# Packing a batch's transform into the first third of its tiles, so that the second third can use two-product values

## The chip, the cores and the metric

The kernel runs on one core of one Trainium2 chip. The metric is the device time of one execution in microseconds (us). The engines are named as in the profile: PE is TensorE (matrix products; PEld its weight loads), DVE is VectorE, ACT is ScalarE, POOL is GpSimd, SP is SyncE, whose queue issues most transfers. PSUM is the accumulator memory that PE writes; this kernel uses all eight of its banks of 128 x 512 float32.

## The reference

Eight batches of 3008 x 256 go through a two-dimensional Fourier transform whose real part is kept, and then row by row through a gated feed-forward layer of width 1536.

```python
def _attn_ref(x):                      # x: (8, 3008, 256)
    X = np.fft.fft(x, axis=1)
    X = np.fft.fft(X, axis=2)
    return X.real.astype(np.float32)

def _moe_ref(x, w_gate, w_val, w_out): # x: (24064, 256)
    gate = np.maximum(x @ w_gate, 0.0)
    val = x @ w_val
    return (gate * val @ w_out).astype(np.float32)
```

## The kernel before

**Transform.** The transform over the 3008 rows is computed as matrix products with tables of sines and cosines. It leaves two bf16 tables for each batch, U (cosine part) and V (sine part), with 128 channels on the partitions and 1505 columns. One column stands for two output rows, which differ only in the sign of V's contribution. The transform over the 256 channels is not computed: it is folded into the weights once, which gives WA (weights for U), WB (weights for V) and WM = -2 WB. The channel in the middle sits in a row of its own, CB, and is added as a bias ("seed") by ACT.

A batch's transform is 24 products of 376 or 377 columns, in four *families* of six: V and U for odd outputs, V and U for even outputs. All families accumulate in one PSUM bank, d (pool psD, one buffer). A family's first three products write d; ACT copies d to the tile es (L598); the next three products add to the same bank; ACT copies the total to the table as bf16 (L601, "whole"); DVE computes the mirrored half as 2 es - d in two instructions of 188 columns each (L603, "half-sums"). Only when both half-sums have read d may the next family, or any other user of d, write the bank.

**Feed-forward.** A batch's columns are cut into three *blocks* of 512, 512 and 481 columns (`thirds`). Each block has 12 tiles of 128 hidden units (`fi`). So a batch from 1 on has 36 *slots*, one call of `slot` for each tile, numbered `at` = 12 block + fi. While the tiles of batch b run, the transform of batch b+1 is computed (`todo_dft`), the input of batch b+2 is folded on POOL (`todo_fold`), and the output products of the block before are spread over the slots (`todo_out`, L784, two per 128 x 512 output bank, evicted by ACT at L797).

A usual tile ("n") has five products. Gate: WM0 V into bank g (L1021), copied by ACT as q (L1024); WA0 U onto a seeded bank p (L1028). DVE forms p - q/2 (L1032) and POOL adds q (L1033): these are the gates of the two rows of a column. Value: WA1 U and WB1 V into a bank v (L876, L877), multiplied by the gate on DVE (L912); then WM1 V is added to the same bank (L882, "mirror"), which turns the value into that of the other row, and DVE multiplies again (L912). The mirror is issued in the next slot, when the tile is `pending`, and waits until the first multiplication has read v.

A *short* tile has two value products instead of three: ACT seeds bank d (L1049), WA1 U is added (L1053), ACT copies twice that (L1054), WV V is added (L1058, WV is half of -WM1). The other row's value is the copy minus d, formed on DVE in place where the tile is `own` (L1065), on DVE in SBUF and multiplied on POOL where it is not (L1067, L1068). A "j" tile has its gate in one bank: WA0 U onto the seeded p (L1028), copied doubled by ACT (L1039), WB0 V added (L1043), copied by ACT (L1044), the difference on POOL (L1045). A *mixed* block has short tiles at fi 2 and 8 and j tiles at fi 5 and 11.

Short tiles need bank d, so they stand where no transform does. Before the change these are the third blocks of batches 2 to 5 (mixed), and in batches 6 and 7, where POOL has less to do, the third block of 6 and all of 7 (short tiles at fi 2, 6, 10, or 2, 5, 8).

**The order of work** is written by hand: engines execute in the order in which the code issues. `slot(cur, mid, nxt, after)` works on tiles fi to fi+3: the first part of the output products, the gate products of `nxt`, the seed of `after`, the mirror of `pending` and its multiplication, the value of `cur` and its first multiplication, L1032 and L1033 of `nxt`, one eviction, one half-sum, the rest of the output products (about 3 of 8). After each slot the batch loop issues `DFT_EVEN[at]` transform steps.

```python
DFT_EVEN = (3, 0, 3, 0, 0, 0) * 4 + (0,) * 12
```

So before the change a family takes six slots, and the four families take the first and the second block. Each list of deferred steps is emptied one step at a time: `evict` holds ACT's copies (the transform's go to its front), `sums` the half-sums. `run_fold` issues POOL's folding steps by a credit of 0.72 us per slot.

Of the kernel before, what the change touches and what calls it, by code (L numbers as in the profile page):

```python
# [34 lines left out]
def kernel(  # L35
# [8 lines left out]
    nc = tc.nc  # L44
    B, S, D = x.shape
# [511 lines left out]
            return dst[:, 0:NJ], dst[:, NJ:2 * NJ]  # L557
        return dst[:, 3 * NJ:4 * NJ + 1], dst[:, 2 * NJ:3 * NJ]

    evict, sums = [], []  # L560

    def flush():
        for todo in (evict, sums):
            while todo:
                todo.pop(0)()

# [3 lines left out]
    def family(b, dst, fam, sine, now=True, pool=None):  # L570

        n, cols = (NE, slice(0, NE)) if fam == 0 else (NJ, slice(NE, NK))
        src, tab = (GG[b % 2], tabS) if sine else (FF[b % 2], tabC)
        st, apart = {}, now or pool is not None

        def mm(par, t, nyq=False):
            if par not in st and not apart and not par:
                st[0] = st[1]  # L580
            elif par not in st:
                home, tag = pool or ((psG, "g") if now and not par else (psD, "d"))
                st[par] = home.tile([128, 512], F32, name=tag, tag=tag)
            rows = slice(0, ROWS[par][t])
            if nyq:
                nc.tensor.matmul(st[par][0:1, 0:n], lhsT=FF[b % 2][rows, fam, t, par, 128:129], rhs=tabC[rows, 2 * t + par, cols],
                                 start=False, stop=(t == 2), skip_group_check=True)
            else:
                nc.tensor.matmul(st[par][:, 0:n], lhsT=src[rows, 1 - fam if sine else fam, t, par, 0:128],  # L589
                                 rhs=tab[rows, 2 * t + par, cols], start=(t == 0 and (apart or par == 1)), stop=(t == 2),  # L590
                                 skip_group_check=not apart)
                if b > 2 and (fam, sine, par, t) == (0, False, 0, 2):
                    widen(st[par], n)

        def end(par):
            if par:
                st["es"] = rp.tile([128, NE], F32, name="es", tag="es", bufs=2)
                evict.insert(0, lambda: nc.scalar.copy(st["es"][:, 0:n], st[1][:, 0:n]))  # L598
            elif not apart:
                whole, rest_ = half_of(dst, fam)  # L600
                evict.insert(0, lambda: nc.scalar.copy(whole, st[1][:, 0:n]))  # L601
                for c in (slice(0, NJ // 2), slice(NJ // 2, NJ)):
                    sums.append(lambda c=c: nc.vector.scalar_tensor_tensor(rest_[:, c], in0=st["es"][:, c], scalar=2.0, in1=st[1][:, c],  # L603
                                                                           op0=ALU.mult, op1=ALU.subtract))
            else:
                for d, op in zip(half_of(dst, fam), (ALU.add, ALU.subtract)):
                    m = d.shape[-1]
                    sums.append(lambda d=d, op=op, m=m: nc.vector.tensor_tensor(d, st["es"][:, 0:m], st[0][:, 0:m], op=op))
            if now:
                flush()  # L610

        def at(par):
            home, tag = pool
            st[par] = home.tile([128, 512], F32, name=tag, tag=tag)
            return st[par]
        return mm, end, at

    def dft_first(U, V):

        raw, ends = [], [family(0, dst, 1, False, now=False, pool=pool) for dst, pool in ((U, (psP, "p")), (V, (psO, "o")))]  # L620
        bank = {(k, par): ends[k][2](par) for k in range(2) for par in (1, 0)}

        def products(t, k, rs):
            src, tab = ((FF[1], tabC), (GG[1], tabS))[k]
            for r, par in [(r, par) for r in rs for par in (1, 0)]:
                rows = slice(0, ROWS[par][t])
                nc.tensor.matmul(bank[k, par][:, 0:NJ], lhsT=src[rows, r, t, par, 0:128], rhs=tab[rows, 2 * t + par, odd_k],
                                 start=(t == 0 and r == 0), stop=(t == 2 and r == 1), skip_group_check=bool(k))

        def nyquist(t):  # L630
            for par in (1, 0):
                rows = slice(0, ROWS[par][t])
                nc.tensor.matmul(bank[1, par][0:1, 0:NJ], lhsT=ny[rows, t, par:par + 1], rhs=tabC[rows, 2 * t + par, odd_k],
                                 start=False, stop=False, skip_group_check=True)

        def combine(i, js):
            for j in js:
                home, tag = ((psV, "v"), (psV, "v"), (psG, "g"), (psD, "d"))[len(raw)]
                p = home.tile([128, 512], F32, name=tag, tag=tag)
                for kc in range(2):  # L640
                    nc.tensor.matmul(p[:], lhsT=(TA, TB)[j][:, kc, :], rhs=wr[i][0][:, kc, :], start=(kc == 0), stop=(kc == 1))
                raw.append(p)

        def whole(W, p):
            return W[:, 0:512], p[:]

        products(0, 0, (0,))
        products(0, 1, (0,))
        whole_128(0)
        angle(4, 5)  # L650
        products(0, 0, (1,))
        products(0, 1, (1,))
        nyquist(0)
        angle(5, 4)
        whole_128(1)
        for T in (TA, TB):
            nc.scalar.copy(T[:, 1, 0::2], T[:, 0, 0::2])
            nc.scalar.mul(T[:, 1, 1::2], T[:, 0, 1::2], -1.0)
        products(1, 0, (0, 1))
        products(1, 1, (0, 1))  # L660
        nyquist(1)
        combine(0, (0, 1))
        nc.scalar.copy(*whole(WA[0], raw[0]))
        whole_128(2)
        products(2, 0, (0, 1))
        ends[0][1](1)
        ends[0][1](0)
        evict.pop(0)()
        nc.vector.tensor_scalar(m2[:], pidx[:], scalar1=1.0, op0=ALU.min, scalar2=-2.0, op1=ALU.mult)
        sums[0]()  # L670
        nc.scalar.copy(*whole(WB[0], raw[1]))
        nyquist(2)
        products(2, 1, (0, 1))
        ends[1][1](1)
        ends[1][1](0)
        evict.pop(0)()
        sums[2]()
        combine(1, (0, 1))
        nc.scalar.copy(*whole(WA[1], raw[2]))
        nc.scalar.copy(*whole(WB[1], raw[3]))  # L680
        for k in (1, 3):
            sums[k]()
        del sums[:]
# [160 lines left out]

    DFT_0 = (0, 0, 0, 0, 0, 3, 0, 0, 4, 3, 3, 0), (0, 0, 0, 0, 0) + (1,) * 7, (3, 3, 3, 3, 3, 3, 0, 0, 0, 0, 0, 0)

    DFT_EVEN = (3, 0, 3, 0, 0, 0) * 4 + (0,) * 12
    DFT_1 = (3, 0, 3, 0, 0, 0) * 4 + (0, 1, 0, 1, 1) + (0,) * 7
    todo_out, todo_dft, todo_fold = [], [], []
    credit, paired = 0, False  # L850
# [8 lines left out]
    def run_one(todo):  # L859
        if todo:  # L860
            todo.pop(0)()
# [136 lines left out]
    def new_tiles():  # L998
        for b in range(1, B):
            for blk, block in enumerate(thirds):  # L1000
                for fi in range(NF):
                    st = tile_of(block, fi, uv[b])
                    st["b"] = b
                    mixed = 1 < b < 6 and blk == 2
                    st["kind"] = "o" if (b, blk, fi) == (1, 0, 6) else "j" if mixed and fi in (5, 11) else "n"
                    st["own"] = mixed
                    st["short"] = mixed and fi in (2, 8) or (b, blk) in ((6, 2), (7, 0), (7, 1)) and fi in SHORT or (b, blk) == (7, 2) and fi in (2, 5, 8)
                    st["lead"] = (b, blk, fi) == (1, 0, 0)
                    yield st

    def seed(st):

        if st is None or st["kind"] == "o":
            return
        st["p"] = bank("p")
        nc.scalar.activation(st["p"][:, 0:st["n"]], st["c"], ACTF.Copy, scale=b2[:, st["fi"]:st["fi"] + 1])  # L1016
# [55 lines left out]
    def slot(cur, mid, nxt, after, outs, fold_us):  # L1072
# [7 lines left out]
            run(todo_out, len(todo_out) - stop + outs * part // 8)  # L1080
        old = nxt is not None and nxt["kind"] == "o"
        new = nxt is not None and nxt["kind"] == "n"
        if old:
            gate(nxt)
        lead = cur["lead"]
# [31 lines left out]
        if lead:  # L1117
            out(5)
            cosine_part(nxt)
            seed(after)  # L1120
        if new:
            both(nxt)
        if old:
# [6 lines left out]
        if nxt is not None and nxt["short"]:  # L1130
            seed_value(nxt)
        run_fold(fold_us)
        if not joined:
            run_one(evict)
        run_one(sums)
        out(8)
        return cur

# [3 lines left out]
    for b in range(B):  # L1142
# [4 lines left out]
        for blk, block in enumerate(blocks):  # L1147
# [72 lines left out]
            else:  # L1220
                for fi in range(NF):
# [1 line left out]
                    cur = ahead.pop(0)  # L1223
                    add_h(cur, hs)
                    ahead.append(next(tiles, None))
                    outs = per_tile + ((-2, 0, -2, 2, 2, 0)[fi % 6] if per_tile == 7 else 0)
                    if (b, blk) == (B - 1, 2) and fi > 8:
                        outs = (10, 9, 19)[fi - 9]
                        if fi == 9:
# [5 lines left out]
                        nc.scalar.mul(WV[:, f], WM[1][:, f], -0.5)  # L1235
                    if (b, at) == (2, 0):
                        nc.sync.dma_start(out=WB[0][0:1, :], in_=WM[0][0:1, :])
                    pending = slot(cur, *ahead, outs, .72)
                    for step in more_1.get(at, ()) if b == 1 else ():
                        step()  # L1240
                    run(todo_dft, DFT_1[at] if b == 1 else DFT_EVEN[at])
# [44 lines left out]
```

## Time and profile before

| | us |
|---|---|
| median of 3 runs | 625.35 (625.21 to 625.96) |
| the profiled execution | 625.38 |
| its span, first to last instruction | 623.5 |
| PE busy | 614.8 (99%) |
| DVE busy | 547.9 (88%) |
| POOL busy | 516.4 (83%) |
| ACT busy | 473.6 (76%) |

The profiled execution is 0.03 us from the median; 1.9 us of it lie outside the span. A timeline row gives the start in us from the beginning of the span, the duration of the whole row in us, the engine, the line of the kernel, the operation, the tiles (out<-in), the shape and how many instructions are merged in the row (x3). A bracket at the end names idle time before it and what ended that. A matmul's row shows its latency, which overlaps with the next one, so PE's pace is read from the distance of starts. A row of the stage table gives, for a stretch of the span, the elapsed time, then each engine's busy time (and instruction count), PE's granted clock, the share of the transfer engines and GB/s. A few matmul records are missing from the trace.

The batches from 1 on begin at about 112 us. Batch 2's three blocks run from 187.05 to 211.50, to 236.97 and to 259.60 us, measured at the start of the last value product of the block's last tile.

### The profile page before, as it was taken

What the parts mean: (1) busy time and instruction counts of PE and PEld (TensorE: products, weight loads), DVE (VectorE), ACT (ScalarE), POOL (GpSimd) and SP (SyncE); (2) the same over time, 40 slices, a digit from 0 to 9 for tenths busy, and PEclk for the clock granted to TensorE, in tenths of its full rate; (3) what the DMA queues carried; (4) which work ended last, traced back from release to release, by engine and by line L of the source; (5) the groups of instructions that cost most, each with busy time, mean ns of one, the idle gap of its engine ahead of it and who ended that gap; (6) DMA issues with size and microseconds to landing.
All of it is one profiled execution on the core that took longest, in us unless ns stands there. A gap on an engine that the chain in (4) does not pass through costs nothing.

```text
span 623.5 us, 12412 instructions
## 1 busy us (share of the span) xinstructions
PE 614.8 (99%) x4043; PEld 396.4 (64%) x4087; DVE 547.9 (88%) x978; ACT 473.6 (76%) x878; POOL 516.4 (83%) x490
## 2 busy tenths in 40 slices
PE   8999999999999999999999999999999999999997
PEld 2566666566666666666666666666666666666666
DVE  8886677999899899988999999999999999999991
ACT  7796667777778778776887778777787768999982
POOL 8988992998899988799879989799886656888881
PEclk9999999999999999999999999999999999999999
DMA  9965658744264427315362425211211111211113
GB/s 241 213 200 135 169 181 92 183 88 144 85 152 143 131 71 178 122 45 167 79 189 69 142 77 120 64 54 49 77 44 55 43 61 37 61 52 53 44 51 104
DMA packets 86034, 66.48 MB, mean 107 GB/s; under 512 B 41639, under 2 KB 69063, under 8 KB 85970
## 3 DMA queue, kind: packets, MB, share of 16 engines
q1 hardware_dynamic: 81384, 60.02, 35.4%
q0 software_dynamic: 3984, 4.92, 4.0%
q8 instruction: 32, 0.52, 0.4%
q10 hardware_dynamic: 602, 0.75, 0.4%
q14 instruction: 32, 0.26, 0.1%
HBM read 41.89 MB, written 34.17 MB: 122 GB/s over the span
## 4 chain that ended last, share of the span: by engine, by line
PE 95%; DVE 1%; POOL 1%; issue 1%; DMA 1%; ACT 0%; DVEq 0%; POOLq 0%; ACTq 0%
PE o L784 38%; PE v L882 10%; PE v L877 10%; PE p L1028 8%; PE g L1021 8%; PE v L876 8%; PE d L589 4%; PE p L882 1%; PE p L876 1%; PE p L877 1%; DMA XG<-in_x_dram,gidx 1%; PE d L1053 1%; PE d L1058 1%; PE o L427 1%; POOL XG L120 1%
## 5 line engine op out<-in xcount | busy, mean ns | idle before, releaser
L1033 POOL TENSOR_TENSOR r<-r 128x512 f32<-128x512 f32 (+1 forms) x243 | 302.7, 1253 | 80.2 <-DVE r L1032 77.3
L784 PE MATMUL o<-wo,h 128*128 128x256 bf16 x2172 | 329.6, 273 | 0.2
L912 DVE SCALAR_TENSOR_TENSOR h<-r,v 128x512 bf16<-128x512 f32 (+1 forms) x462 | 294.3, 675 | 38.2 <-PE v L882 32.3
L784 PEld LDWEIGHTS <-h 128*128 128x128 bf16 x2220 | 216.6, 98 | 110.6 <-issue 0.9
L1016 ACT ACTIVATE p<-CB,b 128x512 f32<-128x512 bf16 (+1 forms) x251 | 172.1, 686 | 51.5 <-DVE r L1032 49.6
L1024 ACT COPY r<-g 128x512 f32<-128x512 f32 (+1 forms) x243 | 140.4, 578 | 48.3 <-PE g L1021 41.5
L1032 DVE SCALAR_TENSOR_TENSOR r<-r,p 128x512 f32<-128x512 f32 (+1 forms) x243 | 163.1, 671 | 0.8 <-ACT r L1024 0.8
L877 PE MATMUL v<-V,WB 128*128 128x512 bf16 (+3 forms) x273 | 100.1, 367 | 2.1
L1028 PE MATMUL p<-U,WA 128*128 128x512 bf16 (+1 forms) x251 | 94.1, 375 | 0.0
L1021 PE MATMUL g<-V,WM 128*128 128x512 bf16 (+1 forms) x243 | 91.2, 375 | 0.2
L882 PE MATMUL v<-V,WM 128*128 128x512 bf16 (+1 forms) x232 | 87.0, 375 | 0.2 <-DVE h L912 0.2
L876 PE MATMUL v<-U,WA 128*128 128x512 bf16 (+3 forms) x237 | 86.4, 365 | 0.0
L901 DVE TENSOR_TENSOR h<-r,v 128x376 bf16<-128x376 f32 (+2 forms) x90 | 46.2, 547 | 16.4 <-PE v L882 10.5
L876 PEld LDWEIGHTS <-WA 128*128 128x128 bf16 x328 | 31.9, 97 | 36.1 <-issue 13.4
L797 ACT COPY os<-o 128x512 f32<-128x512 f32 x92 | 52.5, 570 | 2.9 <-issue 2.9
L198 POOL TENSOR_TENSOR XG<-XG,XD 128x510 f32<-128x510 f32 x42 | 52.9, 1268 | 0.8 <-DMA XG<-xr 0.8
L892 ACT ACTIVATE r<-p 128x376 f32<-128x376 f32 (+1 forms) x80 | 38.3, 487 | 18.0 <-PE p L882 8.6
L877 PEld LDWEIGHTS <-WB 128*128 128x128 bf16 x328 | 31.9, 97 | 31.4 <-ACT WB L680 0.2
L206 POOL TENSOR_TENSOR AA<-XG 128x510 f32<-128x510 f32 x42 | 45.3, 1092 | 0.0
L1021 PEld LDWEIGHTS <-WM 128*128 128x128 bf16 x243 | 23.8, 98 | 5.6 <-issue 0.3
L1028 PEld LDWEIGHTS <-WA 128*128 128x128 bf16 x251 | 24.5, 98 | 3.3 <-issue 0.2
L882 PEld LDWEIGHTS <-WM 128*128 128x128 bf16 x233 | 22.8, 98 | 3.6
(201 smaller groups left out, 534.8 us busy)
## 6 DMA issues: line engine op xcount, KB each, us to landing
out_dram<-os SPq DMA_DIRECT2D x124, 128.0 KB
xr<-in_x_dram SPq DMA_DIRECT2D x12, 768.0 KB
XG<-xr SPq DMA_DIRECT2D x12, 768.0 KB
XD<-in_x_dram SPq DMA_DIRECT2D x15, 512.0 KB
out_dram<-os SPq DMA_DIRECT2D x35, 112.0 KB
XD<-in_x_dram SPq DMA_DIRECT2D x8, 448.0 KB
CB<-ch SPq DMA_DIRECT2D x7, 376.2 KB
out_dram<-os SPq DMA_DIRECT2D x13, 96.0 KB
```

Of the source, the lines that this page charges most:

```text
L198: e.tensor_tensor(XG[p, r, t, ::-1, 1:D], XG[p, r, t, ::-1, 1:D], XD[p, r, t, :, D - 1:0:-1], op=ALU.add)
L784: nc.tensor.matmul(st["p"][0:m, q, :], lhsT=lhs(f), rhs=wo[:, f, :], start=(f == 0 and not (early and q)), stop=(f == NF - 1), skip_group_ ...
L876: nc.tensor.matmul(bank[:, 0:st["n"]], lhsT=WA[i][:, st["f"]], rhs=st["us"], start=True, stop=False)
L877: nc.tensor.matmul(bank[:, 0:st["n"]], lhsT=WB[i][:, st["f"]], rhs=st["vs"], start=False, stop=True)
L882: nc.tensor.matmul(bank[:, 0:st["n"]], lhsT=W[i][:, st["f"]], rhs=v, start=False, stop=True, skip_group_check=True)
L912: nc.vector.scalar_tensor_tensor(half_h(st, sign), in0=st["s"][1 + sign][:, 0:n], scalar=0.0, in1=st["v"][:, 0:n], op0=ALU.max, op1=ALU.mult)
L1016: nc.scalar.activation(st["p"][:, 0:st["n"]], st["c"], ACTF.Copy, scale=b2[:, st["fi"]:st["fi"] + 1])
L1021: nc.tensor.matmul(st["g"][:, 0:n], lhsT=WM[0][:, st["f"]], rhs=st["vs"], start=True, stop=True)
L1024: nc.scalar.copy(q[:, 0:n], st["g"][:, 0:n])
L1028: nc.tensor.matmul(st["p"][:, 0:n], lhsT=WA[0][:, st["f"]], rhs=st["us"], start=False, stop=True, skip_group_check=True)
L1032: nc.vector.scalar_tensor_tensor(sp[:, 0:n], in0=q[:, 0:n], scalar=-0.5, in1=st["p"][:, 0:n], op0=ALU.mult, op1=ALU.add)
L1033: nc.gpsimd.tensor_tensor(sm[:, 0:n], sp[:, 0:n], q[:, 0:n], op=ALU.add)
```

## The change

The transform of batch b+1 is issued within the first block of batch b (for b from 2): a family takes three slots, three products after each of two slots and none after the third. Its two ACT copies have a list of their own, `turned_out`, emptied at the start of a slot; a half-sum is issued in the slot after the first multiplication of `cur`, ahead of L1032; after slot 11 one more is issued. With bank d free, the second blocks of batches 2 to 5 become mixed, and the second block of batch 6 gets short tiles at fi 2, 6 and 10. Output products of a first block are spread by -1, -1, +2 over each three slots, and the folding credit per slot becomes 0.76, 0.54, 0.54 us by block. For batch 1 the order stays. The changes in `flush` and `dft_first` only rename the list.

```diff
     def flush():
-        for todo in (evict, sums):
+        for todo in (turned_out, evict, sums):
             while todo:
                 todo.pop(0)()
...
                 st["es"] = rp.tile([128, NE], F32, name="es", tag="es", bufs=2)
-                evict.insert(0, lambda: nc.scalar.copy(st["es"][:, 0:n], st[1][:, 0:n]))
+                turned_out.append(lambda: nc.scalar.copy(st["es"][:, 0:n], st[1][:, 0:n]))
             elif not apart:
                 whole, rest_ = half_of(dst, fam)
-                evict.insert(0, lambda: nc.scalar.copy(whole, st[1][:, 0:n]))
+                turned_out.append(lambda: nc.scalar.copy(whole, st[1][:, 0:n]))
...
-    DFT_EVEN = (3, 0, 3, 0, 0, 0) * 4 + (0,) * 12
+    DFT_EVEN = (3, 3, 0) * 4 + (0,) * 24
...
-                    mixed = 1 < b < 6 and blk == 2
+                    mixed = 1 < b < 6 and blk > 0
...
-                    st["short"] = mixed and fi in (2, 8) or (b, blk) in ((6, 2), (7, 0), (7, 1)) and fi in SHORT or (b, blk) == (7, 2) and fi in (2, 5, 8)
+                    st["short"] = mixed and fi in (2, 8) or (b, blk) in ((6, 1), (6, 2), (7, 0), (7, 1)) and fi in SHORT or (b, blk) == (7, 2) and fi in (2, 5, 8)
...
         new = nxt is not None and nxt["kind"] == "n"
+        early = cur["b"] > 1
+        if early:
+            run_one(turned_out)
         if old:
             gate(nxt)
...
+        if early:
+            run_one(sums)
         if new:
             both(nxt)
...
         run_fold(fold_us)
-        if not joined:
+        if turned_out and not early:
+            run_one(turned_out)
+        elif not joined:
             run_one(evict)
-        run_one(sums)
+        if not early:
+            run_one(sums)
         out(8)
         return cur
...
-                    outs = per_tile + ((-2, 0, -2, 2, 2, 0)[fi % 6] if per_tile == 7 else 0)
+                    if b < 2:
+                        outs = per_tile + ((-2, 0, -2, 2, 2, 0)[fi % 6] if per_tile == 7 else 0)
+                    else:
+                        outs = per_tile + (0 if blk or b == B - 1 else (-1, -1, 2)[fi % 3])
...
-                    pending = slot(cur, *ahead, outs, .72)
+                    pending = slot(cur, *ahead, outs, .72 if b < 2 else (.76, .54, .54)[blk])
+                    if (b > 1 and at == 11):
+                        run_one(sums)
```

Counted in the two built programs, PE has 11 products (and 11 weight loads) fewer, all of 512 columns: 11 tiles become short (33 value products L876, L877, L882 go, 22 products L1053, L1058 come), and 8 products L1021 are replaced by 8 products L1043. DVE has 980 instructions in both. ACT has 33 more, POOL 3 more.

More of the change, by code (lines that the diff above doesn't have):

```diff
@@ L558, in half_of @@
         return dst[:, 3 * NJ:4 * NJ + 1], dst[:, 2 * NJ:3 * NJ]
-    evict, sums = [], []
+    evict, sums, turned_out = [], [], []
     def flush():
-        for todo in (evict, sums):
+        for todo in (turned_out, evict, sums):
             while todo:
@@ L667, in dft_first @@
         ends[0][1](0)
-        evict.pop(0)()
+        turned_out.pop(0)()
         nc.vector.tensor_scalar(m2[:], pidx[:], scalar1=1.0, op0=ALU.min, scalar2=-2.0, op1=ALU.mult)
@@ L675, in dft_first @@
         ends[1][1](0)
-        evict.pop(0)()
+        turned_out.pop(0)()
         sums[2]()
```

## The prediction

> **What bounds the kernel now.** I read the page first: totals, granted clock, and the chain that ended last.
>
> ```profile
> span 623.5 us, 12412 instructions
> ...
> PE 614.8 (99%) x4043; PEld 396.4 (64%) x4087; DVE 547.9 (88%) x978; ACT 473.6 (76%) x878; POOL 516.4 (83%) x490
> ...
> PEclk9999999999999999999999999999999999999999
> ...
> PE 95%; DVE 1%; POOL 1%; issue 1%; DMA 1%; ACT 0%; DVEq 0%; POOLq 0%; ACTq 0%
> ```
>
> PE is the chain, at the full clock. A busy PE is not PE at its peak, so I then read PE's timeline in a first block, over one slot without transform products and into the next.
>
> ```profile
> 203.40 0.65 PE L589 MATMUL d<-tabS,G 128*128 128x377 bf16 x3
> 203.88 0.38 PE L1021 MATMUL g<-V,WM 128*128 128x512 bf16 x1
> 204.10 0.71 PE L784 MATMUL o<-wo,h 128*128 128x256 bf16 x5
> 204.65 0.38 PE L1028 MATMUL p<-U,WA 128*128 128x512 bf16 x1
> 204.86 0.38 PE L882 MATMUL v<-V,WM 128*128 128x512 bf16 x1
> 205.08 0.38 PE L876 MATMUL v<-U,WA 128*128 128x512 bf16 x1
> 205.29 0.38 PE L877 MATMUL v<-V,WB 128*128 128x512 bf16 x1
> 205.51 0.49 PE L784 MATMUL o<-wo,h 128*128 128x256 bf16 x3
> ...
> 206.60 0.38 PE L1028 MATMUL p<-U,WA 128*128 128x512 bf16 x1
> 206.81 0.38 PE L882 MATMUL v<-V,WM 128*128 128x512 bf16 x1
> 207.03 0.38 PE L876 MATMUL v<-U,WA 128*128 128x512 bf16 x1
> 207.25 0.38 PE L877 MATMUL v<-V,WB 128*128 128x512 bf16 x1
> 207.46 0.49 PE L784 MATMUL o<-wo,h 128*128 128x256 bf16 x3
> 207.79 0.48 PE L589 MATMUL d<-tabS,G 128*128 128x377 bf16 x2
> ```
>
> Starts follow without a gap: four 512-column products take 205.51 - 204.65 = 0.86 us, 0.215 each; three output products 207.79 - 207.46 = 0.33, 0.11 each; three transform products 203.88 - 203.40 = 0.48, 0.16 each. So a PE instruction taken out is worth its pace, and a wait put into PE's order is worth its length. Third, the stages: batch 2's blocks, the second block of batch 6, the first of batch 7.
>
> ```profile
> 187.05:211.50 24.45, 24.32 (x158) 15.54 (x160) 22.50 (x39) 19.15 (x35) 24.45 (x22) 1.00 0.48 159
> 211.50:236.97 25.47, 25.36 (x171) 16.65 (x172) 23.82 (x43) 19.41 (x35) 23.20 (x22) 1.00 0.28 76
> 236.97:259.60 22.63, 22.58 (x152) 14.88 (x153) 20.59 (x35) 17.64 (x32) 17.56 (x15) 1.00 0.60 162
> 503.77:529.25 25.48, 25.38 (x171) 16.65 (x172) 23.83 (x43) 20.06 (x36) 16.52 (x14) 1.00 0.19 60
> 551.64:574.63 22.99, 22.83 (x152) 14.90 (x153) 22.09 (x37) 20.95 (x38) 18.70 (x16) 1.00 0.15 48
> ```
>
> After the elapsed time come PE, PEld, DVE, ACT, POOL. DVE follows PE at 92 to 96%, so where a result of DVE is wanted soon, it is late. How DVE stands in a slot, first without, then with half-sums:
>
> ```profile
> 205.35 1.29 DVE L912 SCALAR_TENSOR_TENSOR h<-r,v 128x512 bf16<-128x512 f32 x2 [0.56 <-PE v L882]
> 206.55 0.68 DVE L1032 SCALAR_TENSOR_TENSOR r<-r,p 128x512 f32<-128x512 f32 x1
> 207.30 1.28 DVE L912 SCALAR_TENSOR_TENSOR h<-r,v 128x512 bf16<-128x512 f32 x2
> ```
>
> ```profile
> 225.81 0.65 DVE L1032 SCALAR_TENSOR_TENSOR r<-r,p 128x481 f32<-128x481 f32 x1
> 226.37 0.34 DVE L603 SCALAR_TENSOR_TENSOR U<-es,d 128x188 bf16<-128x188 f32 x1
> 226.63 1.28 DVE L912 SCALAR_TENSOR_TENSOR h<-r,v 128x512 bf16<-128x512 f32 x2
> 227.83 0.65 DVE L1032 SCALAR_TENSOR_TENSOR r<-r,p 128x481 f32<-128x481 f32 x1
> 228.45 1.26 DVE L912 SCALAR_TENSOR_TENSOR h<-r,v 128x512 bf16<-128x512 f32 x2
> ```
>
> The pair L912 (second multiplication of `pending`, first of `cur`) begins 0.49 us after the mirror starts (204.86 to 205.35; 206.81 to 207.30): the mirror's latency and a semaphore. From the pair's start to DVE's next start are 1.20 us (226.63 to 227.83), from a half-sum to the next 0.26, from L1032 to a pair at once behind it 0.62.
>
> **The change part by part.** *PE work removed:* 11 products of 512 columns, 11 x 0.215 = 2.37 us. The 24 transform products of a batch are moved, not removed; the exchange of L1021 for L1043 in 8 tiles is even.
>
> *The packed families.* This is the step on which the result hangs. Now a family's second half-sum stands in the third slot after the family's first, behind that slot's pair; and at that slot's end stand the next family's first products, which overwrite bank d and so wait for this half-sum. Before, two slots lay between:
>
> ```profile
> 200.81 0.34 DVE L603 SCALAR_TENSOR_TENSOR U<-es,d 128x188 bf16<-128x188 f32 x1
> ```
>
> This family's last half-sum ended at 201.15, and the next family's product began at 203.40 (above). Bank d had been free for over 2 us. In the changed order PE runs from the mirror to the transform product in 207.79 - 206.81 = 0.98 us (three products of 512 columns, three of output; each first-block slot at fi 3, 6 and 9 has exactly three left, with 6 or 7 products in all). DVE needs, from the same mirror: 0.49 to the pair, 1.20 through it, the half-sum's 0.34, and the semaphore back to PE. That last step is read where the mirror itself waits for a multiplication:
>
> ```profile
> 229.44 0.37 PE L1028 MATMUL p<-U,WA 128*128 128x481 bf16 x1
> 229.76 0.36 PE L882 MATMUL v<-V,WM 128*128 128x481 bf16 x1
> ```
>
> The pair that began at 228.45 ended at 229.71, and L882 started 0.05 later. So the transform product can start 0.49 + 1.20 + 0.34 + 0.05 = 2.08 us after the mirror, and PE stands for 2.08 - 0.98 = 1.10 us. That is the lower value, for a DVE that is free when the mirror ends. It isn't: the slot before carries the first half-sum, also between pair and L1032. Counted from that slot's mirror, its pair starts at 0.49, half-sum at 1.69, L1032 at 1.95, and the next pair not before 1.95 + 0.62 = 2.57. The next mirror follows after five products of 512 columns and 8 or 7 output products (no transform products in between): 1.95 us by rows (204.86 to 206.81) with 8, 1.84 with 7. The pair so starts 0.62 or 0.73 after its mirror instead of 0.49, and the wait is 1.10 + 0.13 = 1.23 or 1.10 + 0.24 = 1.34 us.
>
> Nothing else covers it: behind the waiting product on PE stand L1021 of the next tile and the five engines' whole supply, and PE executes in its order. It occurs at the second, third and fourth family of a batch (slots 3, 6, 9; the first finds d long free), in batches 2 to 6, 15 times. The first blocks of batches 2, 4 and 6 spread 84 output products (7 per slot, so 6, 6, 9), those of 3 and 5 spread 96 (7, 7, 10): 9 x 1.34 + 6 x 1.23 = 12.1 + 7.4 = 19.5 us. Bounds: 15 x 1.10 = 16.5 and, with every wait at the larger value, 20.1.
>
> The VectorE: DVE Perf Modes page of the Trainium skill (The DRAIN you can't avoid) says that the next operation doesn't start before the pipeline of the last has emptied. The rows differ: L1032 started at 227.83, the pair's row ended at 226.63 + 1.28 = 227.91. By the page the half-sum would start 0.08 later, and 15 such waits would add 1.2 us; I go by the rows.
>
> *The order within the slot.* ACT's copy of d at a slot's start is put ahead of the copy of q. Bank g is wanted by L1021 a slot later (at least 1.95 us), for one more ACT copy of about 0.48; the seed behind them is used in the next slot. Nothing on PE waits; without that cover each would cost up to 0.48. After a wait of PE these have more time still, so no second stall follows it. The half-sum ahead of L1032 delays the gates by 0.26; they are first used two slots later.
>
> *Mixed second blocks.* PE: 25.47 - 12 x 0.16 - 2 x 0.215 = 23.1 us. DVE: 24 multiplications, 10 L1032 and 2 subtractions, 36 x 0.60 = 21.6; it lost its half-sums. POOL's 10 + 2 gate differences stay 12, less folding. ACT has 6 more operations of about 0.6 and 4 fewer transform copies of 0.48 on its 19.4, 21.1. All fit, as in the third block (22.63 us, DVE 20.59) that has this form with 481 columns. What remains are short waits of the mirror: from mirror to mirror at least 0.49 + 1.29 + 0.05 = 1.83 us, while a slot with five products and 6 output ones brings 5 x 0.215 + 6 x 0.11 = 1.74. Two such slots per new block, eight in all, and two in batch 6: 10 x 0.1 = +1.0. The first blocks of batches 2, 4 and 6 had four such slots each and lose them: 12 x 0.1 = -1.2. Together -0.2; bounds -1.2 (no new ones) and +4 (1 us per new block, if a fourth engine falls behind).
>
> *Folding, queues, output spread:* 0. POOL's steps of 20.8 us credit end after 12 slots at 0.76 and 21.6 at 0.54, in slot 34 of 36; POOL is full in the first block now (24.45 of 24.45) and that block gets longer. SP's rows for V and CB go out after slot 10 instead of 20, when V's half-sums are done, so nothing queues behind them. If a fold came late, the price would be within the +4.
>
> Sum against the profiled execution's 625.38 (0.03 from the median): 625.38 - 2.37 + 19.5 - 0.2 = 642.3 us.
>
> **The rivals.** *The half-sum is in time.* If the wait at bank d is below 2.37 / 15 = 0.16 us, the saving wins, down to 625.38 - 2.37 - 0.2 = 622.8. For this DVE would have to end the half-sum about 1.1 us earlier, for instance by being issued at the end of the slot before. Speaking for it: d is free early now. Against it: the order places it behind the pair, whose start the mirror sets, and the only thing between is 0.33 us of output products.
>
> *The mixed second blocks overload DVE or ACT besides:* DVE stands at 21.6 of 23.1 us, 94%; at 1 us in each of four blocks 642.3 + 4 = 646.3. For it speaks that DVE's pairs already start late after L1032; against it that the third blocks run the same pattern at 91%.
>
> *The waits slow PE's clock.* At 15 places PE stands for 1.3 us; if each cost half pace through the slot behind it (1.95 us from mirror to mirror), the time would be 642.3 + 15 x 1.95 = 671.6. The granted clock row shows 9 throughout, but has no such waits in it; that PE is still busy for four fifths of such a block speaks against. The TensorE: Matmul & The Clock Gate page of the Trainium skill (What's actually happening) halves the clock after an idle window of about 3.4 us: by that rule a stand of 1.3 us has no such effect, and no row of before shows one.
>
> **How the numbers follow.** Forecast 0.82, overload 0.10, in time 0.06, clock 0.02. The time is the forecast's, 642.3. The range goes from 625.4 - 2.4 + 16.5 - 1.2 = 638.3, rounded down to 637.5 for a DVE somewhat quicker than its rows, up to the overload's 646.3; the other two cases lie outside. From the same cases: slower 0.94; of the 0.06 in time, 0.05 faster and 0.01 within 0.2%, about what a measurement of this kernel tells from no change.
>
> **What would show it.** In the first block of batch 2, PE idle 1.1 to 1.4 us ahead of L589, three times, released by DVE's L603, and about 19 us in all on PE <- DVE L603; that block near 24.45 + 1.92 + 4.0 - 0.4 = 30 us (12 more transform products, three waits, four mirror waits fewer), the second near 23.2, the third as before. Batches 1 and 7 unchanged. The prediction is wrong if PE runs through the L589 rows, if the waits stand elsewhere, or if the second blocks stay above 24 us.

## The result, and the profile after

| | before | after |
|---|---|---|
| median | 625.62 us (625.21 to 626.21, 6 runs) | 642.93 us (642.56 to 643.31, 6 runs) |
| span of the profiled execution | 623.5 us | 640.3 us |

The ratio is 1.0276, with a 95% interval of 1.0263 to 1.0290: slower by 17.3 us. The page of the changed kernel, the same rows as before the change:

```profile
span 640.3 us, 12464 instructions
...
PE 616.8 (96%) x4076; PEld 395.8 (62%) x4076; DVE 549.3 (86%) x978; ACT 485.4 (76%) x911; POOL 520.8 (81%) x493
...
PEclk9999999999999999999999999999999999999999
...
PE 81%; DVE 10%; POOL 4%; issue 3%; ACT 1%; DMA 1%; DVEq 0%; POOLq 0%; ACTq 0%
```

PE falls from 99% to 96% of the span, and the chain that ended last, 95% PE before, now passes through DVE for 10%. The clock row is as it was. Who stands for whom is told by the answer for the transform's line L589 (releaser, us in total, times):

```profile
  DVE V L603: 11.3, 10
  DVE U L603: 5.6, 5
```

Fifteen times a transform product waited for a half-sum, where before the change none did. One of them, on PE and on DVE, in batch 2:

```profile
197.92 0.38 PE L882 MATMUL v<-V,WM 128*128 128x512 bf16 x1
...
199.76 0.38 PE L882 MATMUL v<-V,WM 128*128 128x512 bf16 x1
199.98 0.38 PE L876 MATMUL v<-U,WA 128*128 128x512 bf16 x1
200.19 0.38 PE L877 MATMUL v<-V,WB 128*128 128x512 bf16 x1
200.41 0.49 PE L784 MATMUL o<-wo,h 128*128 128x256 bf16 x3
202.06 0.64 PE L589 MATMUL d<-tabC,F 128*128 128x377 bf16 x3 [1.16 <-DVE V L603]
202.54 0.38 PE L1021 MATMUL g<-V,WM 128*128 128x512 bf16 x1
```

```profile
198.40 1.28 DVE L912 SCALAR_TENSOR_TENSOR h<-r,v 128x512 bf16<-128x512 f32 x2 [0.55 <-PE v L882]
199.61 0.34 DVE L603 SCALAR_TENSOR_TENSOR V<-es,d 128x188 bf16<-128x188 f32 x1
199.87 0.68 DVE L1032 SCALAR_TENSOR_TENSOR r<-r,p 128x512 f32<-128x512 f32 x1
200.46 1.28 DVE L912 SCALAR_TENSOR_TENSOR h<-r,v 128x512 bf16<-128x512 f32 x2
201.66 0.34 DVE L603 SCALAR_TENSOR_TENSOR V<-es,d 128x188 bf16<-128x188 f32 x1
```

The second half-sum ends at 201.66 + 0.34 = 202.00, and the transform product that overwrites its bank starts at 202.06. By PE's own pace it was due at 199.76 + 0.98 = 200.74: PE stood for 1.32 us. The bracket says 1.16 because idle time counts from the end of the last product's latency, 0.16 behind its pace; so the sum of the waits is 11.3 + 5.6 + 15 x 0.16 = 19.3 us. DVE was busy without a gap from 198.40 on: its pair at 200.46 came 0.70 after the mirror, delayed by the first half-sum and L1032.

The stages need a correction first. The block boundaries of batch 2 that were told ahead of the result are 10.6 us late on the clock of the views. The lengths hold (24.45, 25.47 and 22.63 us), but the busy times quoted with them, those of batches 6 and 7 too, belong to stretches shifted by that much, and the timeline quoted from 203 to 208 us lies in the second block of batch 2, not in the first; batch 1 begins near 105 us, not 112. Batch 2's three blocks before, in their right places (columns as before):

```profile
176.45:200.90 24.45, 24.26 (x154) 15.22 (x156) 22.79 (x40) 19.60 (x34) 23.61 (x19) 1.00 0.62 170
200.90:226.37 25.47, 25.31 (x167) 16.48 (x169) 23.06 (x40) 18.51 (x33) 23.78 (x25) 1.00 0.38 113
226.37:249.00 22.63, 22.63 (x155) 15.04 (x154) 21.55 (x38) 18.75 (x34) 20.04 (x16) 1.00 0.58 144
```

and after, with the second block of batch 3 as a fourth row:

```profile
176.30:206.23 29.93, 26.46 (x170) 16.34 (x169) 23.72 (x42) 20.92 (x39) 25.71 (x22) 1.00 0.52 143
206.23:229.74 23.51, 23.33 (x157) 15.15 (x156) 22.69 (x38) 19.36 (x35) 21.33 (x21) 1.00 0.36 117
229.74:252.27 22.53, 22.53 (x156) 15.07 (x154) 21.33 (x36) 18.76 (x34) 20.18 (x16) 1.00 0.45 101
283.47:306.96 23.49, 23.31 (x157) 15.15 (x155) 22.69 (x38) 18.95 (x34) 21.24 (x21) 1.00 0.33 100
```

The first block took 24.45 us and takes 29.93, where 30 was forecast: 12 more transform products at 0.16 make 1.9 of the 5.5, and PE idle for 29.93 - 26.46 = 3.47 us is three waits of 1.16 by their brackets. The second block went from 25.47 to 23.51. The loss is in the first blocks.

### The profile page after: what moved, and what is told of

Same layout as the page of the kernel before. It is cut to its first block, busy times and chain, and to the rows that moved or that the text cites. A ratio compares the mean times of both kernels' runs of the same rounds, so it can differ in the third digit from the quotient of the medians.

```text
span 640.3 us, 12464 instructions
## 1 busy us (share of the span) xinstructions
PE 616.8 (96%) x4076; PEld 395.8 (62%) x4076; DVE 549.3 (86%) x978; ACT 485.4 (76%) x911; POOL 520.8 (81%) x493
## 4 chain that ended last, share of the span: by engine, by line
PE 81%; DVE 10%; POOL 4%; issue 3%; ACT 1%; DMA 1%; DVEq 0%; POOLq 0%; ACTq 0%
PE o L784 32%; PE v L882 8%; DVE h L912 7%; PE p L1028 7%; PE v L876 7%; PE v L877 7%; PE g L1021 6%; PE d L589 4%; POOL r L1033 2%; DVE r L1032 2%; PE p L882 1%; PE d L1053 1%; PE d L1058 1%; POOL XG L198 1%; PE p L876 1%
## 5 line engine op out<-in xcount | busy, mean ns | idle before, releaser
L1033 POOL TENSOR_TENSOR r<-r 128x512 f32<-128x512 f32 (+1 forms) x235 | 293.1, 1252 | 96.0 <-DVE r L1032 94.6
L912 DVE SCALAR_TENSOR_TENSOR h<-r,v 128x512 bf16<-128x512 f32 (+1 forms) x440 | 281.1, 674 | 53.8 <-PE v L882 45.0
L1024 ACT COPY r<-g 128x512 f32<-128x512 f32 (+1 forms) x235 | 135.8, 578 | 30.9 <-PE g L1021 27.6
L1032 DVE SCALAR_TENSOR_TENSOR r<-r,p 128x512 f32<-128x512 f32 (+1 forms) x235 | 157.6, 671 | 0.8 <-ACT r L1024 0.8
L877 PE MATMUL v<-V,WB 128*128 128x512 bf16 (+3 forms) x265 | 97.1, 366 | 0.0
L876 PE MATMUL v<-U,WA 128*128 128x512 bf16 (+3 forms) x265 | 97.1, 366 | 0.0
L1028 PE MATMUL p<-U,WA 128*128 128x512 bf16 (+1 forms) x251 | 94.2, 375 | 0.0
L1021 PE MATMUL g<-V,WM 128*128 128x512 bf16 (+1 forms) x235 | 88.2, 375 | 0.2
L882 PE MATMUL v<-V,WM 128*128 128x512 bf16 (+1 forms) x221 | 82.8, 375 | 1.1 <-DVE h L912 1.1
L901 DVE TENSOR_TENSOR h<-r,v 128x376 bf16<-128x376 f32 (+2 forms) x90 | 46.2, 547 | 16.4 <-PE v L882 11.3
L876 PEld LDWEIGHTS <-WA 128*128 128x128 bf16 x317 | 30.9, 97 | 33.8 <-issue 12.3
L877 PEld LDWEIGHTS <-WB 128*128 128x128 bf16 x317 | 30.9, 97 | 30.1 <-ACT WB L680 0.2
L912 DVE SCALAR_TENSOR_TENSOR h<-r,d 128x512 bf16<-128x512 f32 (+1 forms) x47 | 31.4, 667 | 0.0
L598 ACT COPY es<-d 128x377 f32<-128x377 f32 (+1 forms) x30 | 14.2, 473 | 20.0 <-PE d L589 19.1
L589 PE MATMUL d<-tabC,F 128*128 128x377 bf16 (+4 forms) x81 | 17.6, 323 | 11.3 <-DVE V L603 11.3
```

Source lines behind the costliest of these rows:

```text
L876: nc.tensor.matmul(bank[:, 0:st["n"]], lhsT=WA[i][:, st["f"]], rhs=st["us"], start=True, stop=False)
L877: nc.tensor.matmul(bank[:, 0:st["n"]], lhsT=WB[i][:, st["f"]], rhs=st["vs"], start=False, stop=True)
L882: nc.tensor.matmul(bank[:, 0:st["n"]], lhsT=W[i][:, st["f"]], rhs=v, start=False, stop=True, skip_group_check=True)
L912: nc.vector.scalar_tensor_tensor(half_h(st, sign), in0=st["s"][1 + sign][:, 0:n], scalar=0.0, in1=st["v"][:, 0:n], op0=ALU.max, op1=ALU.mult)
L1021: nc.tensor.matmul(st["g"][:, 0:n], lhsT=WM[0][:, st["f"]], rhs=st["vs"], start=True, stop=True)
L1024: nc.scalar.copy(q[:, 0:n], st["g"][:, 0:n])
```

## The experiments

The theory is the one of the prediction: bank d has one buffer, and its second half-sum stands on DVE behind two multiplications that themselves wait for the mirror. The rivals: that the packing as such or the mixed second blocks cost the time, or that the wait is a matter of how much PE work covers it.

**The place of the half-sum.** Three kernels change nothing but where on DVE the half-sum is issued. In e1 the second half-sum comes at the end of the slot that carries the first:

```diff
-                    if (b > 1 and at == 11):
+                    if b > 1 and not blk and fi % 3 == 2:
                         run_one(sums)
```

> The second half-sum of each family is issued at the end of the slot that carries the first, ahead of the next pair of multiplications; all else is as in the changed kernel. Theory (PE waits at bank d for the half-sum behind the pair): counted from that slot's mirror the half-sum now starts at 1.95 + 0.57 = 2.52 us and frees the bank at 2.52 + 0.34 + 0.05 = 2.91, where the next transform product is due at 1.84 + 0.98 = 2.82 or 1.95 + 0.98 = 2.93: all 15 waits go but for 0.1 us, and the time falls from 642.9 to 622.5 to 624, below the kernel before by some 2 us. Rival (the mixed second blocks, or the packing as such, carry the loss): it stays above 635.

Measured 625.35 us, ratio to the kernel before 0.9993 (0.9984 to 1.0002). The 15 long waits went, and with them 17.6 us; in its trace the list of waits has no L589 behind L603 any more. But that isn't all of the 19.3 us of the waits:

```profile
198.74 0.49 PE L784 MATMUL o<-wo,h 128*128 128x256 bf16 x3
199.19 0.64 PE L589 MATMUL d<-tabC,F 128*128 128x377 bf16 x3
```

The transform product was due at 198.74 + 0.33 = 199.07 and starts 0.12 later. So it is at ten places, nine of them in batches 2, 4 and 6, 1.3 us in all. The bank is free at about the moment at which it is wanted. The 1.8 us for 15 such places that the later expectations name was put too high.

In e2 the half-sum stands between the two multiplications of a slot, in e3 behind L1032:

```diff
+        if early:
+            run_one(sums)
         if cur["short"]:
             value_sine(cur)
         else:
             value(cur)
...
-        if early:
-            run_one(sums)
         if new:
             both(nxt)
```

```diff
-        if early:
-            run_one(sums)
         if new:
             both(nxt)
+        if early:
+            run_one(sums)
```

> The half-sum is issued between the two multiplications of a slot instead of behind them. Theory: from the mirror of the slot with the first half-sum, the bank is free at 0.49 + 0.60 + 0.26 + 0.60 + 0.62 + 0.60 + 0.34 + 0.05 = 3.56 us instead of 4.16, so each of 15 waits is 0.60 shorter, -9.0; the first multiplication of cur is 0.26 later, which costs about 0.15 at the mirror after the fourth family, +0.8: 634.7. Rival (the wait is for something else than the place of the half-sum on DVE): 642.9 unchanged.

> The half-sum is issued behind L1032 instead of ahead of it. Theory: from the mirror of the slot with the first half-sum: pair 0.49, L1032 1.69, half-sum 2.25, next pair 2.51, L1032 3.71, half-sum 4.27, bank free 4.27 + 0.34 + 0.05 = 4.66 instead of 4.16: each of 15 waits 0.50 longer, 642.9 + 7.5 = 650.4. Rival: 642.9 unchanged.

Measured 634.60 us (ratio 1.0142, 1.0126 to 1.0157) and 651.41 us (1.0408, 1.0392 to 1.0424). Their waits for the half-sum:

```profile
PE d L589 <- DVE V L603: 3.5, 10, 0.4
...
PE d L589 <- DVE U L603: 1.7, 5, 0.4
```

```profile
PE d L589 <- DVE V L603: 17.1, 10, 1.8
...
PE d L589 <- DVE U L603: 8.6, 5, 1.8
```

One DVE instruction less ahead of the half-sum is worth 8.3 us, one more costs 8.5. Divided by 15 that is 0.55 and 0.57 each, near the 0.60 for which a multiplication (197.78 to 198.38 in e2) or L1032 (201.19 to 201.79 in e3) holds DVE. The rows of the place shown above, in e2 and in e3:

```profile
197.29 0.38 PE L882 MATMUL v<-V,WM 128*128 128x512 bf16 x1
...
199.37 0.38 PE L882 MATMUL v<-V,WM 128*128 128x512 bf16 x1
...
200.86 0.64 PE L589 MATMUL d<-tabC,F 128*128 128x377 bf16 x3 [0.35 <-DVE V L603]
```

```profile
199.51 0.38 PE L882 MATMUL v<-V,WM 128*128 128x512 bf16 x1
...
204.24 0.64 PE L589 MATMUL d<-tabC,F 128*128 128x377 bf16 x3 [1.76 <-DVE V L603]
```

From the earlier mirror to the transform product are 202.06 - 197.92 = 4.14 us in the changed kernel, 200.86 - 197.29 = 3.57 in e2 and 204.24 - 199.51 = 4.73 in e3, where the expectations had 4.16, 3.56 and 4.66. In e2 the bracket alone would say 0.81 less (1.16 to 0.35); 0.24 of that is lost ahead of the later mirror, which itself waits there for the first multiplication. The time follows the half-sum's place in DVE's order, which only the theory asked for.

**Cover on PE.** e6 moves two or three output products of the contested slots from ahead of the mirror to behind the value:

```diff
-        out(4 if lead or nxt is None else 5)
+        out(4 if lead or nxt is None else 2 if early and todo_dft and cur["fi"] in (3, 6, 9) else 5)
```

> In the slots that end at the contested bank (fi 3, 6, 9 of first blocks) two or three more output products are moved from ahead of the mirror to behind the value, where they could cover the wait. Theory (DVE is behind from the slot before, and its chain from there sets the bank): the bank is free 4.16 us after the earlier mirror however PE orders its work, 642.9 unchanged within 1 us. Rival (the wait is the half-sum's delay after its own slot's mirror less the cover): 9 x 0.22 + 6 x 0.33 = 4.0 less, 638.9.

Measured 643.01 us (1.0278, 1.0263 to 1.0294), the changed kernel's time to 0.1. PE, in the place that answers to the one shown above:

```profile
198.21 0.38 PE L882 MATMUL v<-V,WM 128*128 128x512 bf16 x1
...
200.03 0.38 PE L882 MATMUL v<-V,WM 128*128 128x512 bf16 x1
...
200.68 0.71 PE L784 MATMUL o<-wo,h 128*128 128x256 bf16 x5
202.35 0.64 PE L589 MATMUL d<-tabC,F 128*128 128x377 bf16 x3 [0.96 <-DVE V L603]
```

The wait ahead of L589 is 0.2 shorter, but it is no gain: the mirror (200.03) now waits itself for the multiplication, and the transform product starts 202.35 - 198.21 = 4.14 us after the earlier mirror, as in the changed kernel. The expectation's chain gave 4.16. DVE's chain over two slots sets the bank, and PE's order inside it is free.

**The packing without the two-product blocks.** In e4 the second blocks are as before the change; e5 is e4 with e1's edit.

```diff
-                    mixed = 1 < b < 6 and blk > 0
+                    mixed = 1 < b < 6 and blk == 2
...
-                    st["short"] = mixed and fi in (2, 8) or (b, blk) in ((6, 1), (6, 2), (7, 0), (7, 1)) and fi in SHORT or (b, blk) == (7, 2) and fi in (2, 5, 8)
+                    st["short"] = mixed and fi in (2, 8) or (b, blk) in ((6, 2), (7, 0), (7, 1)) and fi in SHORT or (b, blk) == (7, 2) and fi in (2, 5, 8)
```

> The transform is packed as in the changed kernel, but the second blocks of batches 2 to 6 keep their three-product values and two-bank gates. Theory (the loss is the packing's wait; the two-product values give back most of their 11 x 0.215 = 2.37 us in waits of the mirror, 1.7 us more in the five second blocks than before): 642.9 + 2.4 - 1.7 = 643.6. Rival 1 (the saving of PE work is whole): 645.3. Rival 2 (the mixed second blocks carry the loss): below 630.

> As e1, but with the second blocks as before the change: packing with early half-sums alone. Theory: the 15 waits of 0.12 us that e1 has left at the transform product stay, +1.8, the mirror waits of the first blocks of batches 2, 4 and 6 go, and no PE product is saved: e1's 625.35 + 2.4 - 1.7 = 626.0. Rival (the saving of PE work is whole): 627.7.

Measured 643.47 us (1.0283, 1.0268 to 1.0299) and 625.59 us (0.9998, 0.9989 to 1.0007). The whole loss stands without any mixed second block, so they don't carry it. And the packing alone, with its half-sums in time, is the kernel before to within the measurement. The 11 products saved show as about 0.5 us (643.47 against 642.93) and, with early half-sums, as 0.2 (625.59 in e5 against 625.35 in e1), less than the 2.37 us of their pace, and the intervals of the ratios overlap: the gain is small, not settled in size.

**A version in which the bank is free early.** e9 issues both half-sums in the same slot, right behind the pair; e10 makes them one instruction of 376 columns for the batches from 3 on.

```diff
-        if early:
+        while early and sums:
             run_one(sums)
...
-                    if (b > 1 and at == 11):
-                        run_one(sums)
```

```diff
-                for c in (slice(0, NJ // 2), slice(NJ // 2, NJ)):
+                for c in (slice(0, NJ),) if b > 2 else (slice(0, NJ // 2), slice(NJ // 2, NJ)):
```

> Both half-sums of a family are issued in one slot right behind the pair, ahead of L1032; the extra one after slot 11 goes. Theory: from that slot's mirror the bank is free at 1.69 + 0.26 + 0.34 + 0.05 = 2.34 us, where the next transform product is due at 2.82 or 2.93: the waits of 0.12 us that e1 has left go as well, 15 x 0.12 = 1.8: 625.35 - 1.8 = 623.5, 2.2 below the kernel before. Rival (L1032 0.26 later delays the gates, and the time is given back there): 625.4 as e1.

> As e9, with one half-sum of 376 columns in place of two of 188 for the batches from 3 on. Theory: DVE's stretch of two half-sums shrinks from 0.52 to about 0.46 us, 20 times in first blocks, so the pair behind starts 0.06 earlier; where a mirror waits for it (about ten places) that is worth up to 0.6 us: 623.0 to 623.5. Rival: 623.5 as e9, since no wait of PE is left there.

Measured 624.64 us (0.9983, 0.9974 to 0.9992) for e9 and 623.07 us (0.9959, 0.9945 to 0.9972) for e10. e9 gained 0.7 over e1 where 1.8 was expected. Its transform products no longer wait, but other products do; the mirror of the next slot, on PE and with the pair that it waits for on DVE:

```profile
199.58 0.38 PE L1028 MATMUL p<-U,WA 128*128 128x512 bf16 x1
199.88 0.38 PE L882 MATMUL v<-V,WM 128*128 128x512 bf16 x1
```

```profile
198.54 1.28 DVE L912 SCALAR_TENSOR_TENSOR h<-r,v 128x512 bf16<-128x512 f32 x2
```

L882 starts 0.30 after L1028 instead of 0.215, 0.06 after the pair ended (198.54 + 1.28 = 199.82), and the pair was late because two half-sums and L1032 stood ahead of it. The expectation had not counted these mirrors. e10, which shortens DVE's stretch, won 1.6 us where 0.6 at the most was expected; how much of that the traces show is told in the last section. DVE in e10, and PE's next transform product there:

```profile
196.17 1.28 DVE L912 SCALAR_TENSOR_TENSOR h<-r,v 128x512 bf16<-128x512 f32 x2 [0.55 <-POOL r L1033]
197.37 0.54 DVE L603 SCALAR_TENSOR_TENSOR V<-es,d 128x376 bf16<-128x376 f32 x1
197.83 0.68 DVE L1032 SCALAR_TENSOR_TENSOR r<-r,p 128x512 f32<-128x512 f32 x1
198.43 1.28 DVE L912 SCALAR_TENSOR_TENSOR h<-r,v 128x512 bf16<-128x512 f32 x2
```

```profile
198.50 0.65 PE L589 MATMUL d<-tabC,F 128*128 128x377 bf16 x3
199.76 0.38 PE L882 MATMUL v<-V,WM 128*128 128x512 bf16 x1
```

The wide half-sum holds DVE for 0.46 us (197.37 to 197.83) where two took 0.26 each, and frees the bank at 197.91, 0.6 us before the next family begins; the pair ends at 199.71, and the mirror behind it starts at 199.76, 0.05 later: just in time.

**The other parts of the change, measured on e10.** e11 takes the old folding credit, e12 the old spread of output products, e13 the old second blocks, e14 moves one output product less per short tile:

```diff
-                    pending = slot(cur, *ahead, outs, .72 if b < 2 else (.76, .54, .54)[blk])
+                    pending = slot(cur, *ahead, outs, .72)
```

```diff
-                    if b < 2:
+                    if True:
                         outs = per_tile + ((-2, 0, -2, 2, 2, 0)[fi % 6] if per_tile == 7 else 0)
```

```diff
-        outs += cur["short"] + (pending is not None and pending.get("short", False)) - 2 * (mid is not None and mid["short"])
+        outs += (pending is not None and pending.get("short", False)) - (mid is not None and mid["short"])
```

> As e10 (623.07), with the folding credit of the kernel before, 0.72 us per slot in all blocks. Theory (POOL's folding lies beside PE's work, and its results are wanted a batch later): 623.1 within 0.5 us. Rival (POOL, busy 25 of 26 us in a first block, is close to being the bound, and the new pace is part of what the packing needs): 624 or more.

> As e10 (623.07), with the output products spread as in the kernel before. In batches 2, 4 and 6 the slots at fi 2 and 8, which carry a half-sum and no transform products, then have 5 output products instead of 9: 1.63 us of PE work for the next mirror against the 1.83 that DVE needs. Theory: 0.2 us in each of 6 such slots, and 0.1 in the half-sum slots of batches 3 and 5, about +1.5: 624.5. Rival (the spread costs nothing once the bank is free early): 623.1.

> As e10 (623.07), with the second blocks of batches 2 to 6 as in the kernel before (three-product values, two-bank gates). Theory (the mirror waits in the mixed second blocks give back more than half of the 2.37 us of PE work that they save): +0.5 to +1.0, 623.6 to 624.1. Rival (with bank d free early the saving is whole): 625.4.

> As e10 (623.07), with one output product less moved per short tile: the slot ahead of a short tile gives up one product instead of two, and the short tile's own slot takes none. Theory (in e10's second blocks the mirror waits of 0.26 and 0.09 us stand in the slots that gave up two products): one product of 0.11 us more in them takes up to 0.2 us per block with two such slots, 12 blocks: -0.5 to -2: 621 to 622.6. Rival (the wait moves to the short tile's slot): 623.1 or more.

Measured, with the ratio to the kernel before:

| | us | ratio |
|---|---|---|
| e10 | 623.07 | 0.9959 (0.9945 to 0.9972) |
| e11, old folding credit | 623.12 | 0.9958 (0.9945 to 0.9972) |
| e12, old spread | 624.13 | 0.9976 (0.9966 to 0.9985) |
| e13, old second blocks | 623.66 | 0.9967 (0.9955 to 0.9979) |
| e14, one product less moved | 621.02 | 0.9925 (0.9911 to 0.9938) |

The folding credit makes no difference (0.05 us). The new spread is worth about 1 us, near the expectation, the two-product second blocks about 0.6; both differences lie within the intervals of the ratios, so their sizes are not settled. The traces point the same way for the second block of batch 3, in e10, e13 and e14:

```profile
276.12:299.55 23.43, 23.18 (x154) 15.15 (x156) 22.63 (x37) 18.85 (x34) 21.29 (x21) 1.00 0.34 106
```

```profile
275.98:299.52 23.54, 23.38 (x155) 15.36 (x157) 22.87 (x37) 16.42 (x28) 21.29 (x21) 1.00 0.37 117
```

```profile
275.67:298.99 23.32, 23.16 (x154) 15.16 (x156) 22.54 (x37) 18.90 (x34) 21.30 (x21) 1.00 0.36 107
```

Two products fewer would be 0.43 us; the block is 0.11 shorter (23.54 to 23.43). Where the rest goes is seen at the start of e10's second block of batch 2, in the slot that gives up two output products to a short tile, on PE and on DVE:

```profile
205.85 0.38 PE L1028 MATMUL p<-U,WA 128*128 128x512 bf16 x1
206.33 0.38 PE L882 MATMUL v<-V,WM 128*128 128x512 bf16 x1
```

```profile
205.00 1.28 DVE L912 SCALAR_TENSOR_TENSOR h<-r,v 128x512 bf16<-128x512 f32 x2
```

L882 starts 0.48 after L1028 instead of 0.215: it waits for the pair that ends at 206.28. e14 gives that slot one product more. It is 2.0 us faster than e10 and beats both kernels: 621.02 us, 4.7 below the kernel before. Most of its gain lies outside the new blocks, since the rule holds for every short tile of batches 2 to 7.

## Why the prediction was right

**The wait at bank d** was the step on which it hung, and it held in place, count and length. 15 waits on PE for L603 were forecast and found. Their lengths, 1.34 us in batches 2, 4 and 6 and 1.23 in 3 and 5: measured 1.32 in batch 2 (above), and in batch 3 the row

```profile
268.51 0.38 PE L882 MATMUL v<-V,WM 128*128 128x512 bf16 x1
270.70 0.65 PE L589 MATMUL d<-tabS,G 128*128 128x377 bf16 x3 [1.05 <-DVE U L603]
```

gives 2.19 - 0.98 = 1.21. One place differs, the last family of batch 3 (279.08): 1.33, since the mirror ahead of it was late as well. The sum is 19.3 against 19.5. The backlog of DVE from the slot before, which made the difference between 16.5 and 19.5, is shown by e6, where cover on PE bought nothing.

**The removed products** are 2.37 us of PE work by pace. With the new mirror waits of the second blocks, which are the next term, they show as 0.2 to 0.6 us (e5 against e1, e4 against the changed kernel, e13 against e10).

**The mirror's short waits** were the term that was sized worst: -0.2 in all. In the second blocks they took back most of the saving (batch 2: 25.47 before, less 12 x 0.16 and 2 x 0.215, would be 23.12; 23.51 measured, 0.39 above, where 0.2 was put), while the first block of batch 2 lost its own as forecast: 24.45 + 12 x 0.16 + 3 x 1.32 = 30.33, and 0.40 less was measured. Over the whole kernel the two profiled executions leave 642.56 - 625.38 + 2.37 - 19.3 = +0.25 us for the mirrors and all else, where -0.2 was put. The waits at bank d were put 0.2 too high and the mirrors 0.45 too low; that these partly cancel is luck, worth 0.2 us: the forecast was 642.3, the profiled execution took 642.56 and the median is 642.93.

**Nothing elsewhere.** The folding credit cost nothing in e11, which was measured on e10. ACT's new order has no run of its own; that it cost nothing, and that no second stall followed a wait, rests on the sum, which leaves 0.25 us for everything but the waits and the removed products. POOL was not full in the first block, as the prediction read from the shifted row, but at 23.61 of 24.45 us.

**The rivals.** The overloaded second blocks fall by e4. The half-sum in time was a matter of one slot: e1 made it so, and the kernel came down to 625.35, not to 622.8, for one part because 0.12 us was left at ten places, and the mirrors of the second blocks waited as in the changed kernel; the rest was not traced. The slower clock: the granted clock is 1.00 in the blocks with the waits, and the slot behind the wait shown above keeps its pace (202.06 to 202.54 for three transform products, 0.16 each in both kernels). In e3 the stands are 1.9 us and the granted clock is 0.999. By the rule of the TensorE: Matmul & The Clock Gate page of the Trainium skill (What's actually happening) the clock falls after an idle window of about 3.4 us; the traces agree as far as stands of 1.9 us go, and no run here has a longer one at this place.

**The rule against the rows on DVE.** In the DVE rows of the changed kernel the half-sum starts at 201.66, 0.08 before the pair's row ends (200.46 + 1.28 = 201.74), and the sum goes by such starts. The VectorE: DVE Perf Modes page of the Trainium skill (The DRAIN you can't avoid) says that the next operation starts only when the pipeline of the last is empty, and adds that one which isn't held starts earlier. The prediction gave the first half alone, so the page does not contradict the rows. It also priced that half too low: from the earlier mirror to the half-sum DVE starts six times behind another operation, and 0.08 at each would be an estimated 0.48 us for a wait, not 0.08, about 7 us in all. With 4.14 us measured from that mirror where the rows give 4.16, nothing of it is in the time.

## What to carry to other kernels

When steps that share one buffer are packed closer, write down for the buffer's last reader what stands ahead of it on its own engine, and from which event that queue starts; then compare with the work between that same event and the next writer. If the reader's engine is nearly as busy as the engine that bounds (here DVE at 22.79 us against PE's 24.26 in a first block), count back one period further, since its backlog, not the event, may set the start. And a saving on the bound engine is whole only in those periods that are not already as short as another engine's loop allows: in e6, with less PE work ahead of it, the mirror came no sooner than 1.82 us after the one before (198.21 to 200.03).

## What was not expected of the hardware

One DVE instruction of 376 columns held the engine for 0.46 us (its row lasts 0.54) where two of 188 took 0.26 each (rows of 0.34). That is 0.06 us, 20 times, and the median fell by 1.6 from e9 to e10. But it does not reach the end at each of the 20 places. The first products of two families that follow each other in batch 2, in e9 and in e10:

```profile
191.98 0.65 PE L589 MATMUL d<-tabS,G 128*128 128x377 bf16 x3
...
198.56 0.65 PE L589 MATMUL d<-tabC,F 128*128 128x377 bf16 x3
```

```profile
191.99 0.65 PE L589 MATMUL d<-tabS,G 128*128 128x377 bf16 x3
```

With e10's second, at 198.50 (shown with e10), they lie 6.58 and 6.51 us apart. In batch 5, where a slot has one output product more, it is 6.82 in both (410.80 to 417.62; 410.06 to 416.88). So what the DVE instruction is shortened by reaches the end where a mirror waits for DVE, at the families of batches 2, 4 and 6 and at one place in batch 3, and is worth nothing where PE has work enough in the slot. The two profiled spans differ by 1.0 us (622.3 and 621.3); where the other 0.6 of the medians' difference lies was not traced.
